# One token to a partition from pair 2 on, and pair 9's x scaled ahead of pair 10's B and C

## The chip, the cores and the metric

The kernel runs on one core of a Trainium2 chip. The metric is the device time of one execution in microseconds (us), as the median of several runs. Beside it stands one profiled execution, whose trace gives every instruction's start and length; times within it count from the start of its span.

## The reference

A chunked state-space layer (Mamba-2 style) feeds a bilinear feed-forward layer. The sizes are batch 4, 8 heads, 768 tokens, head dimension 32, state size 16; the feed-forward layer has d_model 256 and d_ff 1536.

```python
# per chunk, for every batch and head; cum is the running sum of log(a) in the chunk
M       = (C @ B.T) * exp(cum_i - cum_j) * causal
y       = M @ x + (C @ state) * exp(cum)
state   = exp(cum_last) * state + (B * exp(cum_last - cum)).T @ x
# then, with y as (batch*tokens, heads*head_dim)
out     = ((y @ w_a) * (y @ w_b)) @ w_out          # float32, 3072 x 256
```

## The kernel before

The 768 tokens are cut into 6 blocks of 128 (`NBLK`). In each block the four batches make two pairs, so there are 12 pairs of (block, two batches): pairs 0 and 1 are block 0, pairs 2 and 3 block 1, and so on to pairs 10 and 11. The order of all work is written out by hand; nothing is planned at build time. Each engine runs its own instructions in the order of the program, and waits by semaphores for the others.

For a pair the steps are these. `load1` brings B, C and x of one batch into SBUF; `loads_bc` issues the four loads of C and B of a pair on SyncE's queue and takes the pair's three input buffers (three of each kind rotate), `loads_x` the two of x. `scale_bc` multiplies B or C by factors made from the decays (`factors_mm`, `fb`), `scale_x` turns x into 16 bits. `transposes` turns B and C on TensorE (pairs 0 to 3), or `turn` does it with a DMA transpose on SyncE's queue (pairs 4 on). `scores` multiplies C and B into four PSUM banks `SC`, `mask` multiplies these by the causal mask and writes `T1`, on VectorE or, by way of ScalarE, on GpSimd. `pv_u` multiplies `T1` with x, `ds_mm` makes the sums for the next block's state, `state_sums` and `state_spread` finish the state. The result goes to `X2T` (pairs 0 to 3) or `XB` (pairs 4 on), which the feed-forward units read: `unit` and `out_half` for one pair at a time in blocks 0 and 1, `bunit` and `bout` for a whole block from block 2 on.

Two layouts of the inputs exist. Below pair `P0` = 4 a partition holds two neighbouring tokens of one batch: 64 partitions per batch, and the DMA moves runs of 128 bytes for B and C and of 256 bytes for x. Each product over tokens is then two matmuls over 64 rows. From pair 4 on a partition holds one token of each batch of the pair: 128 partitions, runs of 64 and 128 bytes, and one matmul over 128 rows. The mask for the first layout is `causal`, for the second `causal_q`; both are made by GpSimd, `causal_q` at about 25.5 us.

The queues around the change are as follows. GpSimd issues the loads of pair 2 among those of the weights `Wa`, `Wb` and `Wo`. SyncE waits for the second half of `Wb` and then issues pair 3's B, C and x, pair 4's and pair 5's C and B, pair 4's transpose (`turn`, L331), two output stores, C of pair 6, pair 5's transpose, and so on. Later, in the stage of pair 8, the order that the change touches is:

```python
    bout(2, 0)
    bout(2, 1)
    loads_bc(10)

    stage(8, True, (6, 7))
    prep_x(8)
    prep(10)
```

`prep(10)` is `scale_bc` of C and B of pair 10 on GpSimd and the DMA transpose on SyncE; `prep_x(9)`, `scale_x` of pair 9 on GpSimd, follows inside the loop over the blocks. `group(4)` then multiplies the masked scores of pairs 8 and 9 with their x (L402).

Of the kernel before, what the change touches and what calls it, by code (L numbers as in the profile page):

```python
# [28 lines left out]
def kernel(  # L29
# [25 lines left out]
    NP = NBP * NBLK  # L55
    NG = NBLK - 1
    P0 = 4


    j = np.arange(128)  # L60
# [77 lines left out]

    def load1(eng, p, which, bt, i0=0, n=64):
        blk, bp = divmod(p, NBP)  # L140
        if p >= P0:
            return eng.dma_start(  # L142
                by_token(pair_in[p][which])[:, bt],
                (B, C, x)[which][2 * bp + bt, :, blk * Q : (blk + 1) * Q, :].rearrange("h q n -> q h n"),
            )
        src = (B, C, x)[which][2 * bp + bt, :, blk * Q + 2 * i0 : blk * Q + 2 * i0 + 2 * n, :]
        return eng.dma_start(  # L147
            pair_in[p][which][64 * bt + i0 : 64 * bt + i0 + n].rearrange("i h r n -> i h (r n)"),
            src.rearrange("h (i r) n -> i h (r n)", r=2),
        )  # L150
# [79 lines left out]
    def factors_mm(lo, hi, fps=None, k0=0):  # L230
        if fps is None:
            fps = bank("fps")
        w = 2 * NBP * H
        F = fps[:, k0 * w : (k0 + hi - lo) * w].rearrange("p (k r c) -> p k r c", k=hi - lo, r=2)
        for k in range(lo, hi):
            if k * NBP >= P0:
                for bt in range(2):
                    nc.tensor.matmul(  # L238
                        F[:, k - lo, bt], Pr[:, k], selr[:, k, bt], start=True, stop=True, skip_group_check=True
                    )  # L240
                continue
            for r in range(2):
                for bt in range(2):
                    nc.tensor.matmul(
                        F[64 * bt : 64 * bt + 64, k - lo, r],
                        Pr[:, k].rearrange("p (i r) -> p r i", r=2)[:, r],
                        selr[:, k, bt],
                        start=True,
                        stop=True,
                        skip_group_check=True,  # L250
                        tile_position=(0, 64 * bt),
                    )
        return F.rearrange("p k r c -> p (k r c)")
# [20 lines left out]
    def scale_bc(p, which, eng, factor=None):  # L274
        blk, bp = divmod(p, NBP)
        name, f = (("bm", fB), ("cm", fC))[which]
        raw = by_token(pair_in[p][which]) if p >= P0 else pair_in[p][which].rearrange("p h r n -> p r h n")
        if p >= P0 and which:
            eng.tensor_tensor(  # L279
                out=planes[p % 2][:, 4:6].rearrange("p t (h n) -> p t h n", n=N),  # L280
                in0=raw,
                in1=f[:, blk, :, bp].unsqueeze(3).broadcast_to((128, 2, H, N)),
                op=ALU.mult,
            )
            return
        m_ = mid.tile([128, 2, H, N], f16, name=name, tag=name)
        eng.tensor_tensor(  # L287
            out=m_,
            in0=raw,
            in1=(f[:, blk, :, bp] if factor is None else factor).unsqueeze(3).broadcast_to((128, 2, H, N)),  # L290
            op=ALU.mult,
        )
        st.setdefault(p, {})[name] = m_
        if p >= P0:
            dst = planes[p % 2][:, 0:4].rearrange("p (t e) (m f n) -> p t e m f n", e=2, f=2, n=N)
            for e in range(2):
                eng.tensor_copy(dst[:, :, e, :, e], m_.rearrange("p t (m f) n -> p t m f n", f=2)[:, :, :, e])

    def transposes(p, ps=None, between=None, apart=False):
        s = st[p]  # L300
        if ps is None:
            ps = [SC[0], SC[1]] if apart else None
            on_dve = apart
        else:
            on_dve = True
        TB, TC = (TT[:, 0:256], TT[:, 256:512]) if ps is None else [t_.bitcast(f16)[:, 0:256] for t_ in ps]
        for T_, src in ((TB, s["bm"]), (TC, s["cm"])):
            for r in range(2):
                nc.tensor.transpose(
                    T_[:, r * 128 : (r + 1) * 128], src[:, r].rearrange("p h n -> p (h n)"), ident  # L310
                )
            if between:
                between()
                between = None
        BT = mid.tile([128, 2, 2, 2, 64], f16, name="bt", tag="bt")
        CT = mid.tile([128, 2, Q], f16, name="ct", tag="ct")
        b_ = []
        for e in range(2):
            o_ = BT[:, e].rearrange("p r t i -> p (r t i)")
            b_.append(nc.scalar.activation(out=o_, in_=TB, func=AF.Copy, scale=par[:, e : e + 1]))  # L320
        c_ = (nc.vector.tensor_copy if on_dve else nc.scalar.copy)(
            CT.rearrange("p t (i r) -> p r (t i)", r=2), TC.rearrange("p (r c) -> p r c", r=2)
        )
        if apart:
            for i_ in b_:
                tc.declare_no_dep(c_.ins, i_.ins.name, reason="reads of two banks")
        s["BT"], s["CT"] = BT, CT

# [6 lines left out]
    def scores(p):  # L335
        BT, CT = st[p]["BT"], st[p]["CT"]
        st[p]["T1"] = mid.tile([128, H, 2, Q], f16, name="t1", tag="t1")
        for e, bt, m in itertools.product(range(2), range(2), range(4)) if p >= P0 else ():
            rows = slice(32 * m, 32 * m + 32)
            c0 = (e * 2 + bt) * Q  # L340
            nc.tensor.matmul(  # L341
                SC[m][:, c0 : c0 + Q],
                BT[rows, e, bt],
                CT[rows, bt],
                start=True,
                stop=True,
                skip_group_check=True,
                tile_position=(32 * m, 0),
            )
        for e in range(2) if p < P0 else ():  # L350
            for r in range(2):
                for m in range(4):
                    for bt in range(2):
                        rows = slice(32 * m, 32 * m + 32)
                        c0 = (e * 2 + r) * Q
                        nc.tensor.matmul(  # L356
                            SC[m][64 * bt : 64 * bt + 64, c0 : c0 + Q],
                            BT[rows, e, r, bt],
                            CT[rows, bt],
                            start=True,  # L360
                            stop=True,
                            skip_group_check=True,
                            tile_position=(32 * m, 64 * bt),
                        )

    def product(p, m):

        if p >= P0:
            return (
                st[p]["T1"][:, 2 * m : 2 * m + 2].rearrange("p e t q -> p (e t) q"),  # L370
                SC[m].rearrange("p (c q) -> p c q", q=Q),
            )
        return (
            st[p]["T1"][:, 2 * m : 2 * m + 2].rearrange("p e r q -> p e (r q)"),
            SC[m].rearrange("p (e c) -> p e c", e=2),
        )
# [20 lines left out]

    def pv_u(p, u, py, first):
        s = st[p]
        for bt, g in itertools.product(range(2), range(4)) if p >= P0 else ():  # L400
            c0 = 32 * (g ^ 2 * bt)
            nc.tensor.matmul(  # L402
                py[bt, u][c0 : c0 + 32],
                by_token(s["X16"])[:, bt, u * 4 + g],
                s["T1"][:, u * 4 + g, bt],
                start=False,
# [1 line left out]
                skip_group_check=True,  # L408
                tile_position=(0, c0),
            )  # L410
        for r in range(2) if p < P0 else ():
            for g in range(4):
                for bt in range(2):
                    h = u * 4 + g
# [11 lines left out]
    def ds_mm(p, c0, banks):  # L426
        s = st[p]
        s["DS"] = [b_[:, c0 : c0 + 2 * D] for b_ in banks]
        for bt, m in itertools.product(range(2), range(4)) if p >= P0 else ():
            nc.tensor.matmul(  # L430
                s["DS"][bt][32 * m : 32 * m + 32, :],
                s["bm"][:, bt, 2 * m : 2 * m + 2, :].rearrange("p h n -> p (h n)"),
# [3 lines left out]
                skip_group_check=True,  # L436
                tile_position=(0, 32 * m),
            )
        for r in range(2) if p < P0 else ():
            for m in range(4):  # L440
                for bt in range(2):
                    k = slice(64 * bt, 64 * bt + 64)
# [381 lines left out]
    h = unit(1, 5)  # L824
    scores(2)
    load1(nc.gpsimd, 4, 2, 0)
    mask(product(2, 3), by_pool=True)
    mask(product(2, 0))
    mask(product(2, 1))
    mask(product(2, 2))  # L830
    h()
    scale_x(2, nc.scalar)
    scale_bc(3, 0, nc.gpsimd)
# [61 lines left out]
    def bu(blk, *ks):  # L895
        return [lambda k=k: bunit(blk, k) for k in ks]
# [10 lines left out]
    for bt in range(2):  # L907
        load1(nc.sync, 6, 0, bt)
    loads_bc(7)
    mask(product(3, 0))  # L910
    h()
    for m in range(1, 4):
        mask(product(3, m))
    out_half(1, 0)
    out_half(1, 1)
    go((2, 2))
# [41 lines left out]
    prep(8)  # L958
    prep(9)
    loads_x(9, nc.sync)  # L960
    masked(7, (0, 1, 2), *bu(2, 5, 6, 7, 8, 9, 10, 11))
    group(3)
    bout(2, 0)
    bout(2, 1)
    loads_bc(10)

    stage(8, True, (6, 7))
    prep_x(8)
    prep(10)
    loads_bc(11)  # L970
    loads_x(10, nc.sync)
# [2 lines left out]
    for blk in range(4, NBLK):  # L974
        pB = blk * NBP + 1
        stage(pB, False)
        prep_x(pB)
        loads_x(pB + 2, nc.sync)
        prep(pB + 2)
        masked(pB, (0, 1))  # L980
# [53 lines left out]
```

## Time and profile before

| what | before |
|---|---|
| median of 3 runs | 126.12 us (126.0 to 126.27) |
| the profiled execution, its span | 126.2 us |
| the profiled execution, its own time | 127.94 us |
| TensorE busy | 118.5 us (94%) |
| VectorE busy | 85.3 us (68%) |
| ScalarE busy | 71.8 us (57%) |
| GpSimd busy | 67.3 us (53%) |
| DMA packets, bytes | 63153, 13.73 MB; 57904 of them under 512 B |

In the profile's lines PE is TensorE's matmuls, PEld its weight loads, DVE VectorE, ACT ScalarE, POOL GpSimd and SP SyncE; a q after a name is that engine's sequencer, which issues DMAs. L402 is line 402 of the kernel. A line of a timeline has start, length, engine, line, operation, what is written and read, how many, and in brackets the idle time of the engine before it and what ended that. A line of waits has who waited for what, the total in us, how often, and the longest. A line of the chain has start, length and work. The DMA row shows the mean busy share of the 16 DMA engines in 40 equal slices, in tenths; a line of a DMA queue has packets, megabytes and the share of the 16 engines' time.

### The profile page before, as it was taken

How to read it: one execution, taken by the hardware profiler on the slowest of the kernel's cores; microseconds unless marked ns; L12 is line 12 of the kernel's file. 1: busy time of each engine (PE TensorE's matmuls, PEld its weight loads, DVE VectorE, ACT ScalarE, POOL GpSimd, SP SyncE). 2: the span in 40 equal slices, each digit the busy share in tenths (PEclk: the TensorE clock that was granted, in tenths of full speed). 3: DMA queues.
4: the chain of work that ended last, by engine and by line, in shares of the span. 5: the costliest groups of instructions: out<-in, count | busy, mean ns of one | idle time of the engine just before them, and what ended most of it. 6: DMA issues, size and time to landing. Idle time of an engine off the chain costs nothing.

```text
span 126.2 us, 3757 instructions
## 1 busy us (share of the span) xinstructions
PE 118.5 (94%) x1455; PEld 80.9 (64%) x1455; DVE 85.3 (68%) x162; ACT 71.8 (57%) x142; POOL 67.3 (53%) x113
## 2 busy tenths in 40 slices
PE   6887999999999999999999999499999999999990
PEld 2444889988889788744466464358464675555880
DVE  1785876685887579498984999349689643747200
ACT  0464744793546685887668637192736745657220
POOL 7999799959999379289744923607630000000000
PEclk9999999999999999999999999999999999999999
DMA  3999999997969999599973865369921012010122
GB/s 69 159 146 224 179 200 167 204 147 71 124 74 219 97 86 211 98 153 126 173 72 62 139 120 51 62 68 137 199 85 42 5 42 83 0 47 0 42 88 78
DMA packets 63153, 13.73 MB, mean 109 GB/s; under 512 B 57904, under 2 KB 62672, under 8 KB 63136
## 3 DMA queue, kind: packets, MB, share of 16 engines
q1 hardware_dynamic: 58800, 9.01, 45.5%
q0 software_dynamic: 2336, 4.13, 18.5%
q10 hardware_dynamic: 2000, 0.36, 1.5%
q8 instruction: 11, 0.18, 0.7%
q14 instruction: 6, 0.05, 0.2%
HBM read 11.13 MB, written 3.15 MB: 113 GB/s over the span
## 4 chain that ended last, share of the span: by engine, by line
PE 81%; DMA 8%; POOL 5%; SPq 1%; issue 1%; ACT 1%; DVE 0%; POOLq 0%; ACTq 0%
PE ops L677 16%; PE aps L650 15%; PE bps L650 15%; PE aps L584 9%; PE ops L620 9%; PE bps L584 8%; DMA Wa<-in_moe_w_a_dram 5%; DMA bn<-in_B_dram 2%; PE SC L341 2%; PE SC L402 2%; PE fps L238 1%; SPq L142 1%; POOL x L272 1%; POOL cn L147 1%; PE SC L416 1%; PE SC L356 1%
## 5 line engine op out<-in xcount | busy, mean ns | idle before, releaser
L598 ACT COPY asb<-aps 128x512 f32<-128x512 f32 x72 | 41.9, 587 | 15.0 <-PE aps L650 9.7
L662 DVE TENSOR_TENSOR hkb<-bps,asb 128x512 f16<-128x512 f32 x48 | 32.3, 689 | 12.9 <-ACT asb L598 11.8
L650 PE MATMUL aps<-XB,Wa 128*128 128x512 f16 x96 | 28.6, 379 | 0.0
L650 PE MATMUL bps<-XB,Wb 128*128 128x512 f16 x96 | 28.5, 379 | 0.0
L677 PE MATMUL ops<-Wo,hkb 128*128 128x256 f16 (+1 forms) x204 | 22.5, 267 | 0.0
L677 PEld LDWEIGHTS <-hkb 128*128 128x128 f16 x204 | 18.5, 98 | 3.1
L396 DVE TENSOR_TENSOR t<-SC,causal_q 128x512 f16<-128x512 f32 x26 | 16.7, 683 | 4.9 <-PE SC L341 4.9
L605 DVE TENSOR_TENSOR hk<-bps,asb 128x512 f16<-128x512 f32 x24 | 16.1, 684 | 4.0 <-ACT asb L598 3.6
L650 PEld LDWEIGHTS <-Wb 128*128 128x128 f16 x96 | 9.9, 103 | 11.0 <-issue 0.3
L650 PEld LDWEIGHTS <-Wa 128*128 128x128 f16 x96 | 9.7, 103 | 9.1 <-issue 0.2
L584 PE MATMUL aps<-X2T,Wa 128*128 128x256 f16 x96 | 14.4, 274 | 0.9 <-DMA Wa<-in_moe_w_a_dram 0.7
L689 ACT ACTIVATE osb<-ops 128x256 f32<-128x256 f32 (+1 forms) x16 | 6.0, 377 | 14.4 <-PE ops L677 14.2
L584 PE MATMUL bps<-X2T,Wb 128*128 128x256 f16 x96 | 14.1, 273 | 0.0
L620 PE MATMUL ops<-Wo,hk 128*128 128x256 f16 x96 | 11.6, 273 | 0.0
L272 POOL TENSOR_SCALAR x<-xn 128x512 f16<-128x512 f32 x7 | 10.4, 1490 | 1.6 <-DMA xn<-in_x_dram 1.1
L584 PEld LDWEIGHTS <-Wa 128*128 128x128 f16 x96 | 9.3, 103 | 2.4 <-DMA Wa<-in_moe_w_a_dram 1.2
L584 PEld LDWEIGHTS <-Wb 128*128 128x128 f16 x96 | 9.8, 103 | 0.7
L394 POOL TENSOR_TENSOR t<-tmp,causal_q 128x512 f16<-128x512 f32 x6 | 6.9, 1161 | 6.0 <-ACT tmp L393 5.9
L279 POOL TENSOR_TENSOR planes<-cn,fC 128x256 f16<-128x256 f32 x8 | 5.0, 624 | 9.4 <-DMA cn<-in_C_dram 5.8
L620 PEld LDWEIGHTS <-hk 128*128 128x128 f16 x96 | 8.9, 98 | 1.5 <-DVE hk L605 0.2
L396 DVE TENSOR_TENSOR t<-SC,causal 128x512 f16<-128x512 f32 x13 | 8.2, 683 | 1.7 <-PE SC L356 1.6
L287 POOL TENSOR_TENSOR bm<-bn,fB 128x256 f16<-128x256 f32 x11 | 7.1, 643 | 3.9 <-DMA bn<-in_B_dram 2.1
(94 smaller groups left out, 123.2 us busy)
## 6 DMA issues: line engine op xcount, KB each, us to landing
out_dram<-osb SPq DMA_DIRECT2D x23, 128.0 KB, 2.2
xn<-in_x_dram SPq DMA_DIRECT2D x13, 128.0 KB, 4.0
bn<-in_B_dram SPq DMA_DIRECT2D x20, 64.0 KB, 3.4
xn<-in_x_dram POOLq DMA_DIRECT2D x10, 128.0 KB, 5.0
cn<-in_C_dram SPq DMA_DIRECT2D x18, 64.0 KB, 3.8
Wa<-in_moe_w_a_dram POOLq DMA_DIRECT2D x2, 384.0 KB, 7.1
Wb<-in_moe_w_b_dram POOLq DMA_DIRECT2D x2, 384.0 KB, 8.4
Wo<-in_moe_w_out_dram POOLq DMA_DIRECT2D x2, 384.0 KB, 6.6
```

Of the source, the lines that this page charges most:

```text
L272: eng.tensor_scalar(xo, xi, XS, None, ALU.mult)
L287: eng.tensor_tensor(out=m_, in0=raw, in1=(f[:, blk, :, bp] if factor is None else factor).unsqueeze(3).broadcast_to((128, 2, H, N)), op=AL ...
L394: nc.gpsimd.tensor_tensor(out=o_, in0=tmp, in1=c_, op=ALU.mult)
L396: nc.vector.tensor_tensor(out=o_, in0=i_, in1=c_, op=ALU.mult)
L584: nc.tensor.matmul(ps[:, kk * 2 * Q : (kk + 1) * 2 * Q], W[k // 6][:, f, k % 6 // 3 * 384 : (k % 6 // 3 + 1) * 384].rearrange("p (c kk) -> ...
L598: (nc.vector.tensor_copy if on_dve else nc.scalar.copy)(asb, a_ps)
L605: nc.vector.tensor_tensor(out=s["hk"][:, 2 * k2 : 2 * k2 + 2, :].rearrange("p k q -> p (k q)"), in0=b_ps, in1=asb, op=ALU.mult)
L620: nc.tensor.matmul(o_ps[:, 0:d_model], hk[:, k, bt * Q : (bt + 1) * Q], Wo[:, k, :], start=(k == 0), stop=(k == NK - 1), skip_group_check= ...
L650: nc.tensor.matmul(t_, W[k // 6][:, f, k % 6 // 3 * 384 : (k % 6 // 3 + 1) * 384].rearrange("p (c kk) -> p kk c", kk=3)[:, k % 3], XB[:, b ...
L662: return lambda: nc.vector.tensor_tensor(out=s["hk"][:, k], in0=ps[1], in1=asb, op=ALU.mult)
L677: nc.tensor.matmul(o_ps[:, 0:w], hk[:, k, c * Q : (c + 1) * Q], Wo[:, k, cs], start=(k == 0), stop=(k == NK - 1), skip_group_check=True,)
L689: nc.scalar.activation(out=o_sb[:, 0:w], in_=o_ps[:, 0:w], func=AF.Copy, scale=1.0 / (YS * YS))
```

## The change

A second bound `P1` = 2 takes the place of `P0` wherever the layout of the inputs is chosen, so that pairs 2 and 3 too hold one token of each batch to a partition. They keep the rest of their way: `transposes` on TensorE, `pv` and `X2T`. The copies of the turned B and C, the masks and the matmuls follow the layout. In the stage of pair 8, the loads of pair 10's C and B are issued ahead of block 2's first two output stores, and pair 9's x is scaled ahead of pair 10's C and B; the same call inside the loop is left out for that block.

```diff
     P0 = 4
+    P1 = 2
@@ load1, factors_mm, scale_bc (raw), scores, product, ds_mm: the bound of the layout
-        if p >= P0:
+        if p >= P1:
...
@@ transposes
+        if p >= P1:
+            BT = BT.rearrange("p e r t i -> p (e r t i)").rearrange("p (e t k) -> p e t k", e=2, t=2)
...
-            CT.rearrange("p t (i r) -> p r (t i)", r=2), TC.rearrange("p (r c) -> p r c", r=2)
+            CT if p >= P1 else CT.rearrange("p t (i r) -> p r (t i)", r=2), TC.rearrange("p (r c) -> p r c", r=2)
@@ pv_u
-        for bt, g in itertools.product(range(2), range(4)) if p >= P0 else ():
-            c0 = 32 * (g ^ 2 * bt)
+        for bt, g in itertools.product(range(2), range(4)) if p >= P1 else ():
+            c0 = 32 * (g ^ 2 * bt if p >= P0 else g)
...
-                py[bt, u][c0 : c0 + 32],
+                py[bt, u][c0 : c0 + 32] if p >= P0 else py[bt][c0 : c0 + 32, u * Q : (u + 1) * Q],
@@ the order of the work
-    mask(product(2, 3), by_pool=True)
-    mask(product(2, 0))
+    mask(product(2, 3), by_pool=True, by_token=True)
+    mask(product(2, 0), by_token=True)
...
     loads_x(9, nc.sync)
+    loads_bc(10)
     masked(7, (0, 1, 2), *bu(2, 5, 6, 7, 8, 9, 10, 11))
     group(3)
     bout(2, 0)
     bout(2, 1)
-    loads_bc(10)

     stage(8, True, (6, 7))
     prep_x(8)
+    prep_x(9)
     prep(10)
...
     for blk in range(4, NBLK):
         pB = blk * NBP + 1
         stage(pB, False)
-        prep_x(pB)
+        if blk > 4:
+            prep_x(pB)
```

More of the change, by code (lines that the diff above doesn't have):

```diff
@@ L235, in factors_mm @@
         for k in range(lo, hi):
-            if k * NBP >= P0:
+            if k * NBP >= P1:
                 for bt in range(2):
@@ L276, in scale_bc @@
         name, f = (("bm", fB), ("cm", fC))[which]
-        raw = by_token(pair_in[p][which]) if p >= P0 else pair_in[p][which].rearrange("p h r n -> p r h n")
+        raw = by_token(pair_in[p][which]) if p >= P1 else pair_in[p][which].rearrange("p h r n -> p r h n")
         if p >= P0 and which:
@@ L316, in transposes @@
         CT = mid.tile([128, 2, Q], f16, name="ct", tag="ct")
+        if p >= P1:
+            BT = BT.rearrange("p e r t i -> p (e r t i)").rearrange("p (e t k) -> p e t k", e=2, t=2)
         b_ = []
         for e in range(2):
-            o_ = BT[:, e].rearrange("p r t i -> p (r t i)")
+            o_ = BT[:, e].rearrange("p t k -> p (t k)" if p >= P1 else "p r t i -> p (r t i)")
             b_.append(nc.scalar.activation(out=o_, in_=TB, func=AF.Copy, scale=par[:, e : e + 1]))
         c_ = (nc.vector.tensor_copy if on_dve else nc.scalar.copy)(
-            CT.rearrange("p t (i r) -> p r (t i)", r=2), TC.rearrange("p (r c) -> p r c", r=2)
+            CT if p >= P1 else CT.rearrange("p t (i r) -> p r (t i)", r=2), TC.rearrange("p (r c) -> p r c", r=2)
         )
@@ L337, in scores @@
         st[p]["T1"] = mid.tile([128, H, 2, Q], f16, name="t1", tag="t1")
-        for e, bt, m in itertools.product(range(2), range(2), range(4)) if p >= P0 else ():
+        for e, bt, m in itertools.product(range(2), range(2), range(4)) if p >= P1 else ():
             rows = slice(32 * m, 32 * m + 32)
@@ L349, in scores @@
             )
-        for e in range(2) if p < P0 else ():
+        for e in range(2) if p < P1 else ():
             for r in range(2):
@@ L366, in product @@
     def product(p, m):
-        if p >= P0:
+        if p >= P1:
             return (
@@ L410, in pv_u @@
             )
-        for r in range(2) if p < P0 else ():
+        for r in range(2) if p < P1 else ():
             for g in range(4):
@@ L428, in ds_mm @@
         s["DS"] = [b_[:, c0 : c0 + 2 * D] for b_ in banks]
-        for bt, m in itertools.product(range(2), range(4)) if p >= P0 else ():
+        for bt, m in itertools.product(range(2), range(4)) if p >= P1 else ():
             nc.tensor.matmul(
@@ L438, in ds_mm @@
             )
-        for r in range(2) if p < P0 else ():
+        for r in range(2) if p < P1 else ():
             for m in range(4):
@@ L826 @@
     load1(nc.gpsimd, 4, 2, 0)
-    mask(product(2, 3), by_pool=True)
-    mask(product(2, 0))
-    mask(product(2, 1))
-    mask(product(2, 2))
+    mask(product(2, 3), by_pool=True, by_token=True)
+    mask(product(2, 0), by_token=True)
+    mask(product(2, 1), by_token=True)
+    mask(product(2, 2), by_token=True)
     h()
@@ L909 @@
     loads_bc(7)
-    mask(product(3, 0))
+    mask(product(3, 0), by_token=True)
     h()
     for m in range(1, 4):
-        mask(product(3, m))
+        mask(product(3, m), by_token=True)
     out_half(1, 0)
```

## The prediction

> **What bounds the kernel now.** I read the page's busy table and slices first, then TensorE's waits, then the chain of waits, and last the timelines of GpSimd and SyncE around the places these point to.
>
> ```profile
> PE 118.5 (94%) x1455; PEld 80.9 (64%) x1455; DVE 85.3 (68%) x162; ACT 71.8 (57%) x142; POOL 67.3 (53%) x113
> ...
> DMA  3999999997969999599973865369921012010122
> ```
>
> TensorE is busy 94% of the span. The DMA row is nearly full until about 35 us. So after the start, time is won only by less TensorE work or by removing a TensorE wait, and extra DMA work in the first third is not free. TensorE's waits:
>
> ```profile
> PE SC L402 <- POOL x L272: 1.6, 1, 1.6
> PE SC L210 <- DVE warm L179: 1.2, 1, 1.2
> PE aps L584 <- DMA Wa<-in_moe_w_a_dram: 0.7, 1, 0.7
> ```
>
> The last two belong to the start. The first is one wait, in mid-kernel. GpSimd's timeline shows its cause:
>
> ```profile
> 71.88 1.49 POOL L272 TENSOR_SCALAR x<-xn 128x512 f16<-128x512 f32 x1
> 76.93 0.62 POOL L279 TENSOR_TENSOR planes<-cn,fC 128x256 f16<-128x256 f32 x1 [3.56 <-DMA bn<-in_B_dram]
> 78.32 0.62 POOL L287 TENSOR_TENSOR bm<-bn,fB 128x256 f16<-128x256 f32 x1 [0.77 <-DMA bn<-in_B_dram]
> 79.00 0.52 POOL L297 COPY planes<-bm 128x128 f16<-128x128 f16 x2
> 79.61 1.49 POOL L272 TENSOR_SCALAR x<-xn 128x512 f16<-128x512 f32 x1
> ```
>
> GpSimd scales pair 8's x until 73.37, sits idle 3.56 us for pair 10's C and B, prepares them, and only then (79.61) scales pair 9's x, which TensorE wants at 79.55. Yet that x was issued at 69.38 and 70.01 and takes 4.1 us to land (DMA view, 69 to 71 us): it is there at about 74.1.
>
> In the first half two places count, from the chain:
>
> ```profile
> 42.37 0.33 PE SC L341 x16
> ...
> 45.21 0.34 PE SC L341 x16
> ```
>
> These are the scores of pairs 4 and 5. They read DMA transposes that SyncE issues so:
>
> ```profile
> 35.99 1.31 SPq L331 DMA_TRANSPOSE turned<-planes  x1
> ...
> 39.78 2.19 SPq L331 DMA_TRANSPOSE turned<-planes  x1
> ```
>
> The DMA view of 36 to 38 and of 39 to 41 us gives 4.7 and 4.6 us to landing: 40.7 and 44.4. Slack is 1.7 us for pair 4, only **0.8 us for pair 5**.
>
> **What the Trainium skill says.** "DMA: Bandwidth & Descriptors", section "Why small descriptors are slow (HBM only)", gives each packet a fixed overhead of about 3 cycles, so halving a packet doesn't halve its time. The trace agrees: three DMA views with one packet size each, of 45 to 46 us (64 B), 56.5 to 57.2 (128 B) and 50 to 50.5 (256 B), have
>
> ```profile
> q1 hardware_dynamic: 1506, 0.09, 100.9%
> ```
>
> ```profile
> q1 hardware_dynamic: 884, 0.11, 101.8%
> ```
>
> ```profile
> q1 hardware_dynamic: 364, 0.09, 90.3%
> ```
>
> that is 1506, 1263 and 728 packets per us. The same page, "Issuing engines are not separate DMA queues": DMAs of all engines share the same 16 DMA engines. Agreed: pair 3's B, issued by SyncE at 19.73 behind GpSimd's weights, took 6.6 us against a median of 3.4. Its section "SWDGE vs HWDGE vs iDMA" says GpSimd computes its descriptors in software; agreed, an issue with 512 runs takes 0.70 to 0.74 us (L147), with 1024 runs 0.92 (L142). "TensorEngine Tiling (Array Packing)", "Available Configurations": a 32x64 tile fits eight times, 32x128 four times, so half the matmuls need not be half the time. Agreed: 32 small score matmuls take 0.36 us, 16 large ones 0.33.
>
> **The change, part by part.**
>
> *TensorE, pairs 2 and 3.* From the chain: scores 0.36 to 0.335; products with x 0.35 (L416 x32) to 0.28 (half of L402 x32, 0.56); state sums 0.16 (L443 x16) to 0.055 (half of the 0.11 us between L402's end at 65.23 and 65.34). That is 0.20 per pair, 0.40 for both. The factors of block 1 become 4 records of L238's kind (1.34/12 = 0.11 each, 0.45) for 8 of L244 (0.35): +0.10. TensorE has no wait there, so the net **-0.3 us** counts. Masks (683 ns either way), B, C and x scaling and evictions keep their size; no gain.
>
> *x of pair 9.* Scaled right after pair 8's: it waits on GpSimd for its landing (74.1) and ends at 75.6, before TensorE asks at 79.55. Queued behind it are pair 10's C and B, which in the kernel before began at 76.93, so the 1.49 us lie in the idle stretch. The masks TensorE also needs end by 77.9. The wait goes: **-1.6 us**. Bounds: 0 to -1.6.
>
> *C and B of pair 10.* Four SyncE issues move past two output stores. In place of the first store (70.68, 2.07 us long) stands C's first load; then, at about 0.6 us each, the last B goes at about 74.6 against 75.09 and lands 3.1 us later, at 77.7 against 78.2. Pair 10's transpose comes 0.5 us sooner (82.3 to 81.8), for scores wanted at 84.82 less 1.9, 82.9. The stores go some 4 us later; with four output buffers nobody waits. Zero, 1.1 us of cover. Next late would be pair 11's transpose: landing 91.2 less 0.5, wanted at 93.06 less 1.9, 0.4 us of slack.
>
> *Pair 2's loads (GpSimd's queue).* Six issues at +0.2 us are 1.2 us of GpSimd. B's 0.4 falls into the 0.92 us idle before 13.84; C's and x's 0.8, less 0.26 idle at 19.95, push pair 2's B scaling from 20.65 to 21.2. C landed at about 20.9; its 64 B runs may add 0 to 0.7 us (the 64 packets of up to 4 KB for B and C, at 172 ns, doubled, over 16 engines; I take 0.3). The transposes of pair 2 need it at 24.91, not before 22.6: covered. The new wait, VectorE's mask on causal_q, which ends at 25.8 and then 26.5, is wanted at 27.31: covered by 0.8.
>
> *Pair 3's loads (SyncE's queue), the cost that counts.* B and C: 2 x 2048 packets at 1506/us = 2.72 us for 2 x 1024 at 1263/us = 1.62: +1.10. x: 2048/1263 = 1.62 for 1024/728 = 1.41: +0.21. Sum +1.3 us, +0.3 from pair 2 ahead of it, 1.6; SyncE's own issues get shorter (0.43 to 0.58 for 0.60 to 0.76), which may give some 0.2 back: **1.4 us**. Behind them SyncE issues without a wait between 31 and 36 us: pairs 4 and 5's C and B, then both transposes. Pair 4's then lands at 42.1, wanted at 42.1. Pair 5's lands at 45.8, wanted at 44.9: TensorE waits **+0.9 us**. Bounds: 0 if the queue's gaps (the DMA row is low around 31 and 36 us) take it up; 2.5 if each held issue also lengthens the gap behind it.
>
> Sum: -0.3 - 1.6 + 0.9 = **-1.0 us**. The profiled span is 126.2 us and the median of the runs 126.12, so the span stands for a run, although that profiled execution itself took 127.94 us around it. 126.1 - 1.0 = **125.1 us**.
>
> **Rivals.** (1) The smaller packets are hidden: pair 5's lateness stays below the slack left (0.5). For it: DMA gaps near 31 and 36 us, shorter issues. Against: those gaps follow held issues. Time 126.1 - 1.9 = 124.2. (2) Slower: SyncE's queue slips much further. L142's longest issues last over 2.6 us; with 64 B runs already in pair 3, such holds start earlier. Pair 5's wait must exceed 1.9, so the slip 2.4 us, to lose. With two more holds of 1 us on 1.4 the slip is 3.4, the wait 2.9: 127.1. (3) The change doesn't do what it says: TensorE's wait at 79.5 moves instead of going, for example to pair 11's transpose, which has 0.4 us; a slip of 1.5 us there gives back 1.1: 126.2, no change.
>
> **Numbers.** Forecast 50%, hidden 24%, slower 13%, moved wait 13%. A measurement of this kernel tells about 0.2% (0.25 us) from no change. Forecast and hidden are both faster; of the moved wait I give 8 to no change, 3 to faster, 2 to slower. Faster 77%, same 8%, slower 15%. The range goes from 124.0 (hidden, nothing lost) to 126.4, which leaves out most of the slower case.
>
> **What would show it.** Right: no TensorE wait on L272 near 78 us; x of pair 9 scaled at about 74; pair 3's x landing over a us later; a TensorE wait of some 0.9 us ahead of pair 5's scores (or pair 4's), released by the DMA transpose. No wait there means rival 1; one over 1.9 us rival 2. A new wait of TensorE after 80 us, or a late C of pair 2 that stalls the transposes at 24.9, would make the working wrong.

## The result: slower, and the profile after

| | before | after |
|---|---|---|
| median of 20 runs each | 127.13 us | 129.29 us |
| ratio after to before | | 1.0146 (95%: 1.0104 to 1.0189) |
| span of the profiled execution | 126.2 us | 128.3 us |
| its own time | 127.94 us | 130.04 us |

Forecast was 125.1 us, faster. The change costs some 1.5 to 2%. A second series of the changed kernel (6 runs) gave 1.0182 (1.0099 to 1.0265). Here and in all that follows the ratios leave out runs over 1.5% above the fastest of their kernel (in after one of 201.45 us is among them) and the medians don't, so the two differ, by up to 0.7%.

The page of after, its busy table, DMA row and packet count, answers to the lines that the prediction opened with:

```profile
PE 119.3 (93%) x1371; PEld 80.9 (63%) x1371; DVE 85.4 (67%) x162; ACT 71.8 (56%) x142; POOL 68.4 (53%) x113
...
DMA  3999999978969987699996692388911012010122
...
DMA packets 66224, 13.71 MB, mean 107 GB/s; under 512 B 60976, under 2 KB 65744, under 8 KB 66208
```

TensorE has 84 matmuls fewer, yet the span is 2.1 us longer. There are 3071 packets more than before's 63153. The DMA row hardly differs from before's: a mean share cannot show what comes next. TensorE's waits in after:

```profile
PE SC L344 <- DMA turned<-planes: 1.2, 1, 1.2
PE bps L653 <- ACT asb L601: 1.2, 1, 1.2
PE SC L405 <- POOL t L397: 0.8, 1, 0.8
PE SC L310 <- POOL cm L288: 0.7, 1, 0.7
```

The wait on x of pair 9 is gone, as forecast. Four others have come in this profile, 3.9 us in all, each once and each on another releaser. A second profile of after, of 129.52 us, has the same four, at 1.1, 0.6, 0.7 and 0.9 us. The third, on a mask of GpSimd, is not peculiar to after: a second profile of before, shown further down, has it too. Where they lie is read from a table by stage: window, its length, busy TensorE (matmuls), granted clock, DMA share, GB/s. First before, then after.

```profile
25.00:32.00 7.00, 7.00 (x141) 1.00 0.90 110
...
50.00:62.00 12.00, 12.00 (x115) 1.00 0.88 136
62.00:72.00 10.00, 10.00 (x132) 1.00 0.64 97
72.00:84.00 12.00, 10.39 (x134) 1.00 0.58 82
```

```profile
25.00:32.00 7.00, 6.29 (x93) 1.00 0.87 110
...
50.00:62.00 12.00, 9.97 (x131) 1.00 1.09 149
62.00:72.00 10.00, 8.77 (x119) 1.00 0.84 111
72.00:84.00 12.00, 12.00 (x151) 1.00 0.59 91
```

Between 25 and 84 us TensorE of before is idle only in the stage of pair 9's x (12.00 less 10.39). That of after is idle 0.7 us at pair 3, 2.0 us ahead of the scores of pairs 6 and 7 and 1.2 us at pair 8, and not at all in that stage. The starts of the scores, from TensorE's timeline, give the same as a running sum:

| scores of pair | before | after | after less before |
|---|---|---|---|
| 4 | 42.30 | 42.42 | +0.12 |
| 5 | 45.14 | 45.50 | +0.36 |
| 6 | 52.82 | 54.16 | +1.34 |
| 7 | 57.76 | 60.35 | +2.59 |
| 8 | 68.00 | 71.89 | +3.89 |
| 10 | 84.75 | 86.85 | +2.10 |

The loss is thus not at pair 5, where the prediction put it, but between pairs 5 and 8. By pair 10, 1.8 us of it have come back, for after does not have the 1.6 us wait for pair 9's x. GpSimd's timeline in after shows how that x came early, both scalings (pairs 8 and 9) in one line:

```profile
75.78 3.06 POOL L273 TENSOR_SCALAR x<-xn 128x512 f16<-128x512 f32 x2
```

It ends at 78.84, ahead of pair 10's C (78.92), and TensorE takes it at about 83.

The first cause is on SyncE's queue. Its timeline before, and then after (start, length of the issues, what is loaded; two issues to a line):

```profile
19.73 1.37 SPq L147 DMA_DIRECT2D bn<-in_B_dram  x2
21.20 1.44 SPq L147 DMA_DIRECT2D cn<-in_C_dram  x2
22.77 3.36 SPq L147 DMA_DIRECT2D xn<-in_x_dram  x2
```

```profile
19.06 2.11 SPq L143 DMA_DIRECT2D bn<-in_B_dram  x2
21.28 5.99 SPq L143 DMA_DIRECT2D cn<-in_C_dram  x2
27.38 2.02 SPq L143 DMA_DIRECT2D xn<-in_x_dram  x2
...
37.17 1.32 SPq L334 DMA_TRANSPOSE turned<-planes  x1
...
41.59 2.21 SPq L334 DMA_TRANSPOSE turned<-planes  x1
```

Pair 3's two C loads hold SyncE for 5.99 us where they took 1.44: the issue itself does not end (21.28 to 25.26 for the first). Pair 3's x is issued 4.6 us later than before, and its C lands at 30.69 instead of 27.98, which is TensorE's wait on cm. The two transposes are issued only 1.2 and 1.8 us later, because before's queue is held too, only further down: at pair 3's x (3.36 us for two issues) and at pair 4's and pair 5's B (3.27 and 3.52). In both traces the first long hold comes when 2048 runs of SyncE's queue are waiting (four loads of 512 runs in before, two of 1024 in after), and no packet of that queue moves until about 22.5 us in before and 23 us in after: until then the DMA engines are busy with GpSimd's loads. That the number of waiting runs sets the hold is read from this; no run was made to test it.

### The profile page after: what moved, and what is told of

It reads as the page before. It is cut to its first block, busy times and chain, and to the rows that moved or that the text cites. A ratio compares the mean times of both kernels' runs of the same rounds, so it can differ in the third digit from the quotient of the medians.

```text
span 128.3 us, 3588 instructions
## 1 busy us (share of the span) xinstructions
PE 119.3 (93%) x1371; PEld 80.9 (63%) x1371; DVE 85.4 (67%) x162; ACT 71.8 (56%) x142; POOL 68.4 (53%) x113
## 3 DMA queue, kind: packets, MB, share of 16 engines
q0 software_dynamic: 2336, 4.13, 18.9%
## 4 chain that ended last, share of the span: by engine, by line
PE 56%; DMA 24%; POOL 7%; SPq 4%; ACT 2%; ACTq 2%; issue 2%; DVE 1%; POOLq 0%
PE ops L680 15%; PE aps L653 13%; PE bps L653 13%; DMA xn<-in_x_dram 10%; DMA cn<-in_C_dram 8%; PE aps L587 4%; DMA turned<-planes 4%; PE bps L587 3%; SPq L143 3%; DMA bn<-in_B_dram 2%; PE fps L239 2%; POOL t L397 2%; ACTq L148 2%; PE SC L344 1%; POOL x L273 1%
## 5 line engine op out<-in xcount | busy, mean ns | idle before, releaser
L601 ACT COPY asb<-aps 128x512 f32<-128x512 f32 x72 | 41.7, 588 | 14.0 <-PE aps L653 9.7
L399 DVE TENSOR_TENSOR t<-SC,causal_q 128x512 f16<-128x512 f32 x33 | 21.2, 682 | 6.7 <-PE SC L344 6.1
L680 PE MATMUL ops<-Wo,hkb 128*128 128x256 f16 (+1 forms) x204 | 22.5, 267 | 0.0
L397 POOL TENSOR_TENSOR t<-tmp,causal_q 128x512 f16<-128x512 f32 x7 | 8.1, 1160 | 6.7 <-ACT tmp L396 6.6
L524 ACT ACTIVATE XB<-SC 64x512 f16<-64x512 f32 (+1 forms) x9 | 5.3, 594 | 3.7 <-PE SC L433 3.4
```

The costliest lines, as they stand in the source:

```text
L397: nc.gpsimd.tensor_tensor(out=o_, in0=tmp, in1=c_, op=ALU.mult)
L399: nc.vector.tensor_tensor(out=o_, in0=i_, in1=c_, op=ALU.mult)
L601: (nc.vector.tensor_copy if on_dve else nc.scalar.copy)(asb, a_ps)
L680: nc.tensor.matmul(o_ps[:, 0:w], hk[:, k, c * Q : (c + 1) * Q], Wo[:, k, cs], start=(k == 0), stop=(k == NK - 1), skip_group_check=True,)
```

## The experiments

Two theories went into the first runs: **the short runs** of pairs 2 and 3 (more packets, issues held, all loads late) make the loss; or **the rest of the layout** does (other instructions in pairs 2 and 3). Where the expectations use letters, H is the theory that held issues make the loss, F that the fetches of TensorE's program do, and V that the wait on pair 9's x differs from execution to execution.

**Only pair 9's part.** In before, these lines alone:

```diff
+    loads_bc(10)            # ahead of the two output stores
...
     prep_x(8)
+    prep_x(9)
     prep(10)
...
-        prep_x(pB)
+        if blk > 4:
+            prep_x(pB)
```

> Only the second half of the change: pair 10's C and B loaded sooner and pair 9's x scaled ahead of them; pairs 2 and 3 keep two tokens to a partition. Theory P (the loss is the DMA traffic of pairs 2 and 3's short runs, and the x part gains what its wait was): ratio to before about 0.987 (-1.6 us), no TensorE wait on the scaling of x near 79 us. Rival M (the wait only moves: the x part gains nothing, because pair 10's or 11's transpose is late instead): ratio 1.000 within 0.003, with a new TensorE wait of 1 to 1.6 us after 80 us.

Measured: median 126.03 (22 runs) against 126.83 (43), ratio 0.9983 (0.9957 to 1.001). TensorE's waits no longer name x of L272; 0.3 us each remain, at 49.5 us on a mask and at 52.9 us on a transpose:

```profile
PE SC L402 <- POOL t L394: 0.3, 1, 0.3
PE SC L341 <- DMA turned<-planes: 0.3, 1, 0.3
```

So the wait can be removed, but what that brings is 0.8 us by medians and not resolved by the ratio, not the 1.6 us of theory P. The ratio is the one that rival M gave, but M's new wait after 80 us did not come.

**Only the layout.** The changed kernel with pair 9's lines put back as in before:

```diff
-    loads_bc(10)            # back to its place behind the output stores
...
-    prep_x(9)
...
-        if blk > 4:
-            prep_x(pB)
+        prep_x(pB)
```

> Only the first half of the change: one token of each batch to a partition from pair 2 on; the stage of pair 8 stays as it was. Theory P: ratio to before about 1.027 (the whole change's +1.8 us, plus the 1.6 us that the x part gained in it). Rival M: about 1.015, as the whole change, since the x part gave nothing.

Measured: 129.19 (6 runs), ratio 1.0197 (1.0136 to 1.0258). That lies between P's 1.027 and M's 1.015, with M inside the interval. The loss is all here, and the whole change (129.29) is no better: within it, pair 9's part has no visible gain.

**The whole change, old runs.** One bound in `load1` put back, so that loads of pairs 2 and 3 move 128 and 256 bytes; the values of these two pairs then stand in another order than the products take them.

```diff
     def load1(eng, p, which, bt, i0=0, n=64):
...
-        if p >= P1:
+        if p >= P0:
```

> The whole change, but the loads of pairs 2 and 3 keep the old runs of 128 and 256 bytes, which places their data for the old layout; so the values of blocks from 1 on are not the reference's, while every instruction outside these DMAs is the changed kernel's. Theory P (short runs): ratio to before 0.985 (-0.3 us of TensorE, -1.6 us of the x wait). Rival L (the loss is in the compute of the new layout: its masks wait for causal_q, its products come in another order): stays near 1.015.

Measured: 127.35 (22 runs), ratio 1.0022 (0.9986 to 1.0058). Without its short runs the change is not to be told from before. Rival L's 1.015 is excluded, and so is theory P's 0.985, which had counted pair 9's part at the full 1.6 us.

**Before, with short runs.** The opposite, before with another bound in `load1` alone; the values of pairs 2 and 3 again stand in an order that the products don't take them in, here and in the next two and in the one with ScalarE.

```diff
-        if p >= P0:
+        if p >= 2:
```

> The kernel before, but the loads of pairs 2 and 3 move runs of 64 and 128 bytes as in the changed kernel, which places their data for the new layout; so the values of blocks from 1 on are not the reference's, and only these DMAs differ from before. Theory P: ratio to before 1.027 to 1.03, as the layout change alone, with SyncE's later loads 1 to 3 us late. Rival L: 1.000.

Measured: 129.21 (6 runs), ratio 1.0182 (1.0123 to 1.0241). The short runs alone make the whole loss, with no other instruction changed; P had put it higher by about the gain that it expected of pair 9's part. Among TensorE's waits are the one on cm that after has and one that after does not have:

```profile
PE SC L309 <- POOL cm L287: 1.3, 1, 1.3
...
PE bps L584 <- ACT osb L632: 1.2, 1, 1.2
```

The second stands just ahead of pair 5's scores (47.66 us). ScalarE's timeline shows what it had waited for itself, an output store of SyncE's late queue that still held its buffer, and then pair 5's x:

```profile
42.98 0.38 ACT L632 ACTIVATE osb<-ops 128x256 f32<-128x256 f32 x1 [1.30 <-DMA out_dram<-osb]
45.69 0.63 ACT L270 ACTIVATE x<-xn 128x512 f16<-128x512 f32 x1 [2.33 <-DMA xn<-in_x_dram]
```

In before ScalarE waits there for neither. In after it waits 2.60 us for that store, at 43.25, without TensorE waiting for it.

**Pair 3's short runs, pair 2's short runs.** The same line of before, once for each pair:

```diff
-        if p >= P0:
+        if p >= 3:                # pair 3 alone
```

```diff
-        if p >= P0:
+        if p == 2 or p >= P0:     # pair 2 alone
```

> The kernel before with the short runs in pair 3's loads alone, on SyncE's queue (values of blocks from 1 on not the reference's). Theory S (SyncE's queue is held by its own longer descriptor lists): nearly all of the +2.4 us, at least +1.8. Rival G (pair 2's short runs on GpSimd's queue push the weights and all behind them): +1.0 or less.

> The kernel before with the short runs in pair 2's loads alone, on GpSimd's queue (values of blocks from 1 on not the reference's). Theory S: 0 to +0.4 us. Rival G: +1.4 us or more.

Measured: pair 3 alone 128.14 (6 runs), ratio 1.0126 (1.0049 to 1.0202); pair 2 alone 127.90 (22 runs), 1.0099 (1.006 to 1.0138); before 126.71. Either costs about 1.2 to 1.4 us, so neither theory came as it was put: S had at least 1.8 us for pair 3 and at most 0.4 for pair 2, G at most 1.0 and at least 1.4. Pair 2's part, on GpSimd's queue, had been priced at nothing but 0.3 us in the DMA queue.

**The hold by itself.** Which is it, the added packets or SyncE being held? Before with its old runs, and pair 3's second C load (and all that SyncE issues after it) made to wait for pair 2's first x (`c3` and `x2` are these two pairs of loads):

```diff
+    tc.add_manual_dep(c3[1].ins, x2[0].ins.name, AFTER, reason="pair 3's second C after pair 2's first x")
```

> The kernel before with all its old runs; only SyncE's second load of pair 3's C, and all that SyncE issues behind it, waits until pair 2's first x load has landed (about 25.7 us, where it went out at 21.9). Theory H (what costs is that SyncE's queue is held: in the changed kernel that load goes out at 25.3 and pair 3's x from 27.4): +1.0 to +2.0 us to the median of before, with no packet added. Rival B (what costs is the DMA engines' time for more packets): +0.5 us or less, since SyncE's queue catches up.

Measured: 128.46 (22 runs) against 126.78 (35), ratio 1.0098 (1.0055 to 1.0141). SyncE's timeline:

```profile
20.77 5.29 SPq L147 DMA_DIRECT2D cn<-in_C_dram  x2
26.16 1.28 SPq L147 DMA_DIRECT2D xn<-in_x_dram  x2
```

The second C load goes out 3.6 us later than in before (25.47 for 21.89). A hold of about the length seen in after costs 1% with not one packet more, as theory H had it. Where that 1% is lost the trace does not say: this profiled execution took 127.51 us, below the median of its kernel, and its transposes of pairs 4 and 5 were issued only 0.2 and 0.4 us later than in before. ScalarE waits 1.4 us for an output store in it, as with short runs, but TensorE does not wait for that.

**C of pair 3 through ScalarE.** If the hold were all, taking the held issues off SyncE should help. Before with short runs, those two loads issued by ScalarE:

```diff
+    for bt in range(2):
+        load1(nc.scalar, 3, 1, bt)     # ahead of block 1's factors on ScalarE
...
-        load1(nc.sync, 3, 1, bt)
```

> The kernel before with the short runs of pairs 2 and 3 (values of blocks from 1 on not the reference's), but pair 3's two C loads are issued by ScalarE ahead of its copy of the factors at about 21 us, and not by SyncE. The packets are those of the kernel with short runs (129.21 us). Theory H: SyncE goes on to x sooner; 0.8 to 1.6 us of the +2.4 come back, unless ScalarE is held in its stead and delays TensorE. Rival B: 129.2 within 0.4.

Measured: 129.40 (6 runs), ratio 1.0154 (1.0102 to 1.0206), against 1.0182 for the kernel that it was made from. Nothing is recovered that can be told from the noise; theory H's 0.8 us or more did not come. SyncE is now held at x, which has taken C's place behind B:

```profile
18.66 2.19 SPq L142 DMA_DIRECT2D bn<-in_B_dram  x2
21.01 6.46 SPq L142 DMA_DIRECT2D xn<-in_x_dram  x2
```

So the hold falls on whatever is issued behind the 2048 runs of the two B loads. I take it for the sign of a full queue, which moving one issue does not empty; that is argued, not shown.

**The fetches of TensorE's program.** In after, pair 7's and pair 8's transposes take 5.3 and 4.6 us from issue to landing; in before 3.0 and 2.8. The DMA view of after for 54.1 to 59.9 us (a slice is 0.145 us) shows a hole in nearly all traffic, from 56.9 to 58.3 us. It opens while one packet of an "instruction" queue moves (56.4 to 57.3) and outlasts it:

```profile
DMA  4589999999999999987000001100089999999999
...
q8 instruction: 1, 0.02, 1.0%
...
turned<-planes SPq DMA_TRANSPOSE x1, 5.3
```

The same view of before, 52 to 57 us (a slice is 0.125 us), has no such packet:

```profile
DMA  9510000000158999999998998106656897888999
...
turned<-planes SPq DMA_TRANSPOSE x1, 3.0
```

It does have a hole, at its left, from 52.4 to 53.2 us: that one comes just behind before's own packet of 50.6 us (1.6 us long), which fell on pair 6's transpose.

These packets are 16 KB each. Before has 11 of them for TensorE's 2910 matmuls and weight loads, after 10 for 2742, so about one for some 270, and I take them for fetches of TensorE's program. The change takes its 168 instructions (161 by my count of the program, as in the first expectation below) away early, and so moves the later packets: between 40 and 75 us from 41.7, 50.6, 61.7 and 70.6 us to 48.4, 56.4 and 69.4, that is, from the transposes of pairs 5 and 6 into those of pairs 7 and 8. That was a theory of its own, and I tried it in three ways. The first cut the matmuls of pairs 2 and 3 in two halves, which brings them to 2902; one kernel with old runs, one with short.

```diff
+        parts = 2 if P1 <= p < P0 else 1
+        w = Q // parts
...
-                CT[rows, bt],
+                CT[rows, bt, i * w : i * w + w],
```

> The whole change with the old runs of the loads of pairs 2 and 3 (so the values of blocks from 1 on are not the reference's), and each score, product and state-sum matmul of pairs 2 and 3 cut in two halves of its columns, which gives TensorE as many instructions as the kernel before, in the same places. Theory F (with 161 fewer TensorE instructions the fetches of its program fall on the DMA transposes of pairs 7 and 8, which then take 5 us to land and not 3): those transposes land in about 3 us again, and the median falls from 127.35 to about 126.0, that of the x part alone. Rival C (the new layout's compute or its waits cost the 1.3 us): stays at 127.3.

> The changed kernel with each score, product and state-sum matmul of pairs 2 and 3 cut in two halves of its columns, so that TensorE's program is as long as before; the values stay right. Theory F: the short runs' loss of some 2.4 us stays, the fetches' loss goes as far as the two do not hide each other: median 128.0 to 128.8 against 129.3 for the changed kernel. Rival C: 129.3 to 129.6.

Measured: old runs 126.00 (22 runs), ratio 0.9994 (0.9964 to 1.0023); short runs 128.18 (6 runs), 1.0188 (1.0115 to 1.0261). In both the two transposes land after 2.8 to 3.4 us. By medians both forecasts came; by the ratios nothing has changed (0.9994 for 1.0022 with old runs, 1.0188 for 1.0182 with short).

The second put 48 more matmul and weight-load instructions into the warm-up of the kernel with pair 9's part alone, whose pair 6 transpose takes 4.65 us:

```diff
-    warmup(6, SC[3])
+    warmup(24, SC[3], 128)
...
-    warmup(2, SC[3])
+    warmup(8, SC[3], 128)
```

> The x part alone (pair 10's C and B sooner, pair 9's x scaled first), with eight of the warm-up matmuls at the start cut in four each, 48 more TensorE instructions in the same warm-up time, so that each fetch of its program comes some 2 us earlier: from 50.5, inside pair 6's transpose, to about 48.5. Theory F: pair 6's transpose lands in 3 to 3.5 us and not 4.7, and the median is 0 to 0.4 us under the 126.03 of the x part alone. Rival: no effect, or another transpose is hit instead (pair 4's, 35 to 40 us).

Measured: 126.07 (14 runs), ratio 0.997 (0.9935 to 1.0005), as the kernel that it was made from. A miss, since the packet moved by only 1.1 us (50.5 to 49.4) and the transpose still took 4.5 us.

The third moved the packets alone: 82 small matmuls for two large ones in the warm-up, which brings the count to 2902 too and leaves all later stages as they are, each beside its own neighbour on one chip.

```diff
-    warmup(6, SC[3])
+    warmup(4, SC[3])
+    for i in range(82):
+        m, bt = i % 4, i // 4 % 2
+        nc.tensor.matmul(
+            SC[m][64 * bt : 64 * bt + 64, 0:128],
+            warm[32 * m : 32 * m + 32, 0:64],
+            warm[32 * m : 32 * m + 32, 0:128],
...
+            tile_position=(32 * m, 64 * bt),
+        )
```

> The changed kernel as it is, as the neighbour of the padded one. Every theory: some 2.2 us above the kernel before; transposes of pairs 7 and 8 landing about 5 us after their issue.

> The changed kernel with 80 more matmuls in TensorE's warm-up at the start (two 512-column ones give way to 82 of 32x64 by 128 columns), so that its program is as long as before's up to every later stage; pairs 2 and 3 and all loads stay as changed. Fetch theory (the shorter program has moved the fetches of TensorE's program onto the transposes of pairs 7 and 8): fetches back at about 41.7, 50.6, 61.7 and 70.6 us, those two transposes land after about 3 us, TensorE's wait on pair 8's transpose (1.2 us) goes, and the time is 0.7 to 1.2 us below the neighbour's. Theory that the split kernels won by chance or by their other matmuls: the same time as the neighbour within 0.3 us.

> The changed kernel with the loads of pairs 2 and 3 left in their old runs of 128 and 256 bytes (their values then stand in another order than the products take them), as the neighbour of the padded one. Every theory: about 127.35 us, 0.5 above the kernel before.

> Its neighbour (old runs) with the same 80 warm-up matmuls. Fetch theory: transposes of pairs 7 and 8 back to about 3 us, and 1.0 to 1.35 us below the neighbour, at about 126.1. Theory of chance or of the split matmuls: within 0.3 us of the neighbour.

Measured, with before at 126.44 (27 runs):

| | median | ratio to before |
|---|---|---|
| after | 129.03 (6 runs) | 1.0182 (1.0099 to 1.0265) |
| after, padded | 128.16 (6 runs) | 1.0151 (1.0086 to 1.0217) |
| old runs | 126.68 (14 runs) | 0.9993 (0.9944 to 1.0041) |
| old runs, padded | 126.40 (14 runs) | 1.0044 (1.0006 to 1.0083) |

The two neighbours lie 2.6 and 0.2 us above before by medians, where 2.2 and 0.5 were expected.

In the traces the padding does what the theory says. Old runs unpadded have

```profile
PE SC L344 <- DMA turned<-planes: 0.9, 1, 0.9
PE bps L653 <- ACT asb L601: 0.8, 1, 0.8
```

and padded neither; pair 8's transpose takes 3.4 us for 4.3. With short runs it takes 3.1 for 4.6 and both waits go too, but the one on osb comes that before with short runs has, just ahead of pair 5's scores (ScalarE waited 1.5 us for an output store and 2.0 for pair 5's x):

```profile
PE bps L587 <- ACT osb L635: 1.1, 1, 1.1
```

In time, though, only 0.9 us (short runs, forecast 0.7 to 1.2) and 0.3 us (old runs, forecast 1.0 to 1.35) of the medians go, and the ratios overlap, with old runs in the opposite order. Some of the gain may be spent by the padding itself, which starts the first factor matmuls at 4.7 us instead of 4.13. So the effect is **not shown** in time.

**Before once more.** A second profile of before, to see how steady the wait on pair 9's x is.

> The kernel before, unchanged, for a second profile. Theory V (the wait for pair 9's x differs from run to run, and the profile of before caught a long one): a wait of TensorE on the scaling of pair 9's x clearly under 1.6 us, with the span shorter by about as much. Rival: 1.6 us again, within 0.2.

Measured: 127.65 us, span 125.9. TensorE's waits:

```profile
PE SC L402 <- POOL t L394: 1.0, 1, 1.0
PE SC L402 <- POOL x L272: 0.6, 1, 0.6
```

TensorE loses 1.0 us at 50 us, waiting for a mask of GpSimd, so it comes to pair 9's x later and waits 0.6 us instead of 1.6. It goes on at 80.85, where it went on at 81.15 in the first profile, almost the same moment. The wait is thus shorter by 1.0 us, as theory V had it, but the span by 0.3 us only.

## Why the prediction was wrong

*Pair 3's loads, +0.9 us.* **This is the step that failed.** The slip of SyncE's queue was added up from packets (1.4 us) and set against the slack of the transposes of pairs 4 and 5. The transposes did slip by 1.2 and 1.8 us, near the forecast. But TensorE did not wait at pair 5, because it came there 0.36 us late and pair 5's transpose landed in 3.8 us instead of 4.6, at 45.34 for scores at 45.50. The cost came elsewhere, at pair 3's own C (0.7) and then at a mask, at ScalarE and at pair 8's transpose. For this queue slack had been worked out only for the two DMA transposes, while pair 3's C, all that GpSimd prepares and issues behind it, and the output stores were late too: GpSimd scaled C at 29.74 in before, and in after it landed only at 30.69. Nor did SyncE's issues get shorter, by which the sum took 0.2 us back: the first B went out in 0.41 us, but from the second on they are held.

The forecast wait at pair 5 was missed narrowly. In before with short runs, with pair 3's alone and in after padded, TensorE does wait 1.1 to 1.2 us just there, for ScalarE, and pair 5's transpose lands within 0.2 us of those scores' start (47.50 for 47.66, 46.60 for 46.65, 46.75 for 46.95), so that it would have held TensorE for about a microsecond anyway. Measured, pair 3's short runs cost 1.3% (0.5 to 2.0%), some 1.6 us.

*Pair 2's loads, 0 and +0.3 in the queue.* Mis-sized: 1.0% (0.6 to 1.4%), about 1.25 us. The step looked at who waits for pair 2's own data, and that was covered, but its packets lie ahead of pair 3's loads, which share the DMA engines. With pair 2's short runs alone SyncE's issues of pair 3's B and C, in their old runs, take 1.87 and 2.62 us for 1.37 and 1.44. Where the 1.25 us goes is not seen, since that profile is of its kernel's fastest run (126.41 us). Both pairs together, 1.8%, are the whole loss; the sum had 0.9 us, and measured are some 2.3.

*The rival.* Rival 2, at 13%, was right that holds of SyncE's issues start earlier in the queue. Two holds of 1 us were put into it; they were 4.0 and 2.0 us. But it too put the loss at pair 5's transpose, with a slip of 3.4 us, and in after that slipped by 1.8. The Trainium skill's "DMA: Bandwidth & Descriptors", section "Why small descriptors are slow (HBM only)", which the prediction named for the cost of a packet, agrees in direction: the kernel whose loads move the same bytes in half as long runs took longer. No run here ties the hold's length to a figure of that page.

*x of pair 9, -1.6 us.* The order on GpSimd was right, and the wait went. The size was not: 1.6 us was one execution's wait, 0.6 another's. In before this wait takes up what earlier stages lose, since x is ready at the same time whatever TensorE did before. It is therefore worth at most what is left of it, by the ratio 0.4% at most where nothing else is late (0.8 us by medians), and the lost time of after ate into it: 3.89 us late at pair 8, 2.10 at pair 10.

*TensorE, -0.3 us, and C and B of pair 10, 0.* Nothing contradicts them: the whole change with old runs measures 0.9993 and 1.0022. A gain of 0.3 us is below what these runs tell. Pair 10's transpose was no wait in after.

*A term that was missing.* Fewer instructions on TensorE also move the fetches of its program. In the traces of after two of the four new waits go with them (pair 8's transpose, and ScalarE's on pair 6's x, which was issued at 53.37 and landed at 58.56, behind the hole). With the fetches put back these two waits go (and with short runs another comes); how much time goes with them the runs do not settle.

*The base.* The span of 126.2 us was taken for a typical run of 126.12. But a run lasts 1.7 us longer than its span, and the later series of before have medians of 126.4 to 127.1: the three runs shown lie below that, and the profiled one above. Of the 4.2 us between 125.1 and 129.29, about 1.0 is the base, and the other 3.2 are a gain of 1.0 that did not come and a loss of 2.2 that did.

**What stays open.** Why the issue of a load is held is not shown, only that it is while SyncE's earlier runs still wait or drain. Where the 1% of the hold alone is lost is not seen in its trace, and how the 1.8% of the short runs divides into late issues and the packets' own time is not shown, since no kernel has the packets without the hold. No version beats before by more than the interval; the nearest are pair 9's part alone (0.9983) and the same with the warm-up cut finer (0.997, up to 1.0005).

## What to carry to other kernels

Halving the runs of a load can cost more than the time of its extra packets: here, while the runs waited and drained, the issuing engine's next DMA instruction didn't end (4.0 us), and everything behind it in that queue was late. So work out the slack of every later consumer of the queue, output stores and the issues of other engines included, not only of the ones nearest the bound. A single wait in mid-kernel can be a buffer for what earlier stages lose, as the one for pair 9's x was: look at it in more than one execution before its length is taken for a gain. Try the parts of a change apart; here the layout's loads were the loss, and nothing else in it was to be seen in the time.

## What was not expected of the hardware

A queue of kind "instruction" moves 16 KB packets while the kernel runs, in before and after one of 0.9 to 1.6 us for some 270 instructions of TensorE. Where such a packet fell on the transpose of pair 7 or 8, that took 4.3 to 5.3 us from issue to landing in nine cases and 3.4 in one (pair 8's with only the layout), and 2.8 to 3.5 where it was clear of one; in the views shown almost nothing else moves for 0.9 and 1.4 us. Pair 7's was hit in all five traces of the three kernels with fewer instructions; in the four kernels brought back to 2902 pair 8's took 3.1 to 3.4 us. So the place of a packet depends on how many instructions stand ahead of it. That the packet makes the stop, and by what means, is argued from this and not shown by itself; transposes also took over 4 us with no packet inside them, as pair 4's in before (4.66 us from 35.99).
